# A recurrence fused with a convolutional feed-forward block on one Trainium2 core: diagonal term moved to TensorE, weight conversion in three operations, smaller loads

## The chip, the cores and the metric

The kernel runs on one core of a Trainium2 chip. The metric is the device time of one execution in microseconds. A core has five engines that run side by side and wait for each other through semaphores: TensorE (PE in the profile, its weight loads PEld), VectorE (DVE), ScalarE (ACT), GpSimd (POOL) and SyncE (SP), which issues all DMAs of this kernel in one queue.

## The reference

```
for t in range(S):                                   # B, H, S, D = 4, 8, 768, 48
    cur     = einsum('bhd,bhe->bhde', u * k[t], v[t])
    y[:,:,t]= einsum('bhd,bhde->bhe', r[t], state + cur)
    state   = w * state + einsum('bhd,bhe->bhde', k[t], v[t])
x   = y as (B, S, 384)
h   = maximum(x @ w_in, 0)                            # 384 -> 1024
c   = sum over k of conv_w[k] * h shifted by k - 1    # 3 taps along the tokens
out = (h * sigmoid(c)) @ w_out                        # 1024 -> 384
```

The weights w_in, conv_w and w_out come as float64 and are converted on the chip; r, k, v, w, u are float32.

## The kernel before, in words

**Recurrence.** Tokens go in chunks of 64; two chunks are a group of 128 tokens, a batch has 6 groups, all four batches 24. Heads go in four pairs: head A on partitions 64 to 111, head B on 0 to 47. For each group `load(g)` issues DMAs for `KR` (k and r with the head dimension on the partitions), `KRT` (k and r with the tokens on the partitions) and `WW` (the values v in blocks, with rows of zeros, beside the place of the state). `prep(g)` multiplies `KR` by powers of the decay (tables `TK`, `TR`), moves r into `RA` and `RB`, and forms the diagonal term: r times u, times k (two products over `KRT`), then a VectorE sum over the head dimension into `QQ`. GpSimd's affine select puts `QQ` on the diagonal of `RA`/`RB`. `scores(g)` ("sc" below) is 16 products into PSUM `psC`; VectorE's predicated copy puts the part below the diagonal into `RA`/`RB`. `step(g, c)` of each chunk has the state product "S" (8 products into `psS`, copied by ScalarE into the next chunk's `WW`) and the output product "av" (8 products into `psY`). `yout(g)` copies y, moves parts of it between partitions by small DMAs, and splits it into a high and a low part in `XT`.

**Feed-forward.** A batch is two units of about 384 tokens, eight units in all. Each unit has 8 steps. `first(i)`, "f1" below: nine products of 128 output features (`HP`, two PSUM buffers), then on ScalarE relu and the middle tap, on VectorE the two outer taps (`CV`), a sigmoid, the gate product (`SG`), and the split into `GH` and `GL`. `second(i)`, "f2": nine products into three output banks `PO`. So there are 64 f1 and 64 f2.

**Weights.** `convert` takes the words of a float64 as pairs of 32-bit integers. ScalarE scales the upper word read as a float (`CC`); VectorE puts the word together in `TT` with three operations: one takes the sign bit, one shifts the scaled part in, one ORs in bits of the lower word. A rounded high part and the remainder go to `wi`/`wo`. There are 17 pieces: 8 of w_in, 8 of w_out and a small one.

**Order.** `Plan` lists all operations with estimated durations and the data they read and write. A list schedule written in Python orders them before the build; it also chooses between VectorE and GpSimd for the operations marked "any". Every engine then issues its instructions in that fixed order. Where the plan has TensorE resting before the first f2, it puts in "fill" products of zeros (`wz`, 128x256, line 653; the writes go to a bank that is overwritten later). In the profile, nearly all VectorE and GpSimd products bear the line of the helper `tt`, L288.

Of the kernel before, what the change touches and what calls it, by code (L numbers as in the profile page):

```python
# [5 lines left out]
F32 = mybir.dt.float32  # L6
# [7 lines left out]
# choices of the schedule  # L14
DR = 2
# [12 lines left out]
OFF = {  # microseconds by which classes of operations come earlier  # L28
# [15 lines left out]
NBUF = 3  # L44
# [10 lines left out]
U = 386                 # most tokens of a unit of the FFN  # L55
PAT = {"2": [(0, 382), (382, 386)], "s": [(0, 384), (384, 384)]}  # units of a batch: first token, tokens
UNITS = [(b,) + x for b in range(B) for x in PAT[UP[b]]]
NU = len(UNITS)
WS = 256.0              # the weights on chip are scaled by this


class Plan:
    """Operations in a valid order, with the resources they take and the data they read and write. They are
    issued in the order of a list schedule: each engine takes, of what can start, what the tensor engine's
    sequence needs first."""
# [3 lines left out]
    def __init__(self):  # L69
        self.ops = []  # L70
        self.last_w, self.last_r = {}, {}

    def op(self, eng, dur, rd, wr, fn, cls="", x=0.0):
        """x: of a transfer, its time on the DMA engines; of matrix products, the columns they count for the clock."""
# [18 lines left out]
        self.ops.append((dur, x, sorted(pred), fn, cls))  # L93
        return n
# [18 lines left out]
    def order(self):  # L113
# [22 lines left out]
        while todo:  # L136
# [30 lines left out]
            if e == "pe":  # L167
                # zero products where the engine would rest and its clock with it
# [19 lines left out]
                if att and cls not in ATT:  # L188
                    free[e] += 0.065
# [8 lines left out]
                # the part of the block before the end of the tick  # L198
# [13 lines left out]
            elif e == "sp":  # L212
                free[e] = s + d + 0.04
                dq = max(dq, s + d + 0.65) + x
# [3 lines left out]
            else:  # L218
                free[e] = s + d
# [17 lines left out]
LAT, LPE = 0.15, 0.21  # L237
ATT = ("th", "sc", "S", "av")


def rwkv_ffn_kernel(tc, krd, krt, vt, wd, ut, w_in, conv_w, w_out, out):
# [4 lines left out]
    with ExitStack() as ctx:  # L246
# [14 lines left out]
        KRT = sb([128, 2, NP, 2, D], F32, "KRT", NBUF)  # L261
# [22 lines left out]
        def tt(eng, n, rd, wr, cls="", **kw):  # L284
            d = {"dve": dve(n), "pool": pool(n)}
            if eng != "any":
                d = {eng: d[eng]}
            op(eng, d, rd, wr, lambda e: e.tensor_tensor(**kw), cls)  # L288
# [5 lines left out]
        wz = sb([128, 512], BF16, "wz")  # L294
        wc = sb([112, NP], F32, "wc")
        uu = sb([128, NP, D], F32, "uu")
# [10 lines left out]
        dma([], ["wc"], wc, wd)  # L307

# [7 lines left out]
        def load(g):  # L316
            i = g % NBUF
            dma([], [("KR", i)], KR[i], krd[g], 0.45, 1.27, "ldK")
# [4 lines left out]
        dma([], ["uu"], uu, ut)  # L323
# [20 lines left out]
        # powers of the decay: PW[j] = w^j, TK = w^(31-j), TR = w^(j-32), DN = w^(95-j)  # L344
# [19 lines left out]
        op("dve", 0.53, ["PW"], ["PW2"], powers2)  # L364
        op("act", 0.32, ["PW", "PW2"], ["DN"], lambda e: A.copy(DN, PW[:, :, 95:31:-1]))
# [22 lines left out]
        ncv = [0]  # L388

        def convert(src, n, dst, view, keys):  # L390
# [5 lines left out]
            op("act", act(n), [("ST", i)], [("CC", i)],  # L396
               lambda e: A.activation(cc, s2[:, :, 1].bitcast(F32), AF.Copy, scale=2.0 ** -111))
# [319 lines left out]
```

## Time and profile before

| | us |
|---|---|
| median of three runs (344.40 to 347.00) | 344.52 |
| span of the profiled execution | 343.2 |
| first f1 starts in the profiled execution | 50.57 |
| TensorE's last product ends | 339.86 |
| busy: PE, DVE, ACT, POOL | 311.8, 270.4, 206.5, 193.7 |

The profile has no separate time of its execution beside the span; the median of the runs lies 1.3 us above the span, and this distance is taken for what lies around it. The page's busy times overlap: a matmul counts as busy while it goes through the array, though the next has started. The rows of one engine in order of time show how far apart starts are. Each TensorE product of float32 operands appears there as two rows.

### The profile page before, as it was taken

Reading aid. Unit: us, or ns where it says so; the run is one execution under the profiler, and the core shown is the slowest. Engines: PE = TensorE matmul, PEld = TensorE weight load, DVE = VectorE, ACT = ScalarE, POOL = GpSimd, SP = SyncE. Lnnn points to the kernel's source line nnn. Section 1 sums busy time; section 2 is a strip of 40 time slices with the busy share of each in tenths; the row PEclk is TensorE's granted clock in tenths of the full one; section 3 lists DMA queues with packets and bytes.
Section 4 is the critical chain, followed back from the end, with each engine's and each line's share of the span. In section 5 each row is a group of like instructions: output and inputs, shape, how many; then the busy total and the mean of one; then the engine's idle time right before and its main releaser. Section 6 shows DMA issues by size and latency. Waiting matters only on the chain.

```text
span 343.2 us, 8886 instructions
## 1 busy us (share of the span) xinstructions
PE 311.8 (91%) x3487; PEld 285.1 (83%) x3487; DVE 270.4 (79%) x409; ACT 206.5 (60%) x468; POOL 193.7 (56%) x200
## 2 busy tenths in 40 slices
PE   8698694997779988999998999899999999999996
PEld 4486474896668988899997999898999999999995
DVE  6899989989999999978778786786775756565550
ACT  4343446584765765567575663685566755876752
POOL 5998998697899988727455463333231212243230
PEclk9768969698998999999999999999999999999999
DMA  7996975977864297365566571544530200200101
GB/s 192 328 261 166 289 216 173 304 181 218 262 196 124 55 313 214 97 201 165 149 181 174 147 217 50 145 141 135 157 96 13 72 1 2 77 5 1 71 0 70
DMA packets 23882, 50.25 MB, mean 146 GB/s; under 512 B 4448, under 2 KB 10848, under 8 KB 23840
## 3 DMA queue, kind: packets, MB, share of 16 engines
q1 hardware_dynamic: 23840, 49.69, 50.0%
q8 instruction: 27, 0.44, 0.6%
q14 instruction: 15, 0.12, 0.1%
HBM read 36.30 MB, written 4.72 MB: 120 GB/s over the span
## 4 chain that ended last, share of the span: by engine, by line
PE 53%; DVE 17%; POOL 8%; issue 7%; DMA 7%; ACT 6%; SPq 1%; DVEq 0%; POOLq 0%; ACTq 0%
PE HP L569 20%; PE PO L598 19%; DMA KR<-in_krd_dram 4%; PE psC L477 4%; PE psY L507 3%; DVE CV L577 3%; PE psS L493 3%; POOL KRT L288 2%; DVE KR L288 2%; ACT SG L580 2%; DVE RB L481 2%; POOL RA L462 1%; DVE KRT L288 1%; DVE RA L481 1%; PE PO L653 1%
## 5 line engine op out<-in xcount | busy, mean ns | idle before, releaser
L569 PE MATMUL HP<-XT,wi 128*128 128x386 f32 (+2 forms) x576 | 116.1, 347 | 5.0 <-DVE SG L581 5.0
L598 PE MATMUL PO<-GH,wo 128*128 128x384 f32 (+2 forms) x384 | 111.6, 345 | 4.1 <-POOL wo L288 3.3
L569 PEld LDWEIGHTS HP<-XT,wi 128*128 128x128 f32 x576 | 103.4, 192 | 8.5 <-DVE SG L581 4.9
L288 POOL TENSOR_TENSOR GL<-SG,GH 128x384 fp32r<-128x384 f32 (+2 forms) x50 | 53.5, 1070 | 97.5 <-ACT GH L583 87.1
L577 DVE SCALAR_TENSOR_TENSOR CV<-HP,cw,CV 128x384 f32<-128x384 f32 (+2 forms) x128 | 78.2, 614 | 25.4 <-ACT CV L574 23.5
L598 PEld LDWEIGHTS PO<-GH,wo 128*128 128x128 f32 x384 | 71.0, 189 | 6.5 <-POOL wo L288 3.9
L598 PE MATMUL PO<-GL,wo 128*128 128x384 f32 (+2 forms) x192 | 65.3, 340 | 0.0
L580 ACT ACTIVATE SG<-CV 128x384 f32<-128x384 f32 (+2 forms) x64 | 33.5, 524 | 45.8 <-DVE CV L577 45.4
L581 DVE TENSOR_TENSOR SG<-HP,SG 128x384 f32<-128x384 f32 (+2 forms) x64 | 35.5, 555 | 21.1 <-ACT SG L580 20.4
L573 ACT ACTIVATE HP<-HP 128x386 f32<-128x386 f32 (+2 forms) x64 | 30.5, 477 | 23.2 <-PE HP L569 22.5
L583 ACT CAST GH<-SG 128x384 fp32r<-128x384 f32 (+2 forms) x64 | 32.8, 512 | 13.7 <-DVE SG L581 13.7
L500 ACT COPY WW<-psS 48x192 f32<-48x192 f32 x88 | 27.3, 311 | 20.3 <-PE psS L494 15.6
L288 DVE TENSOR_TENSOR KR<-KR,TKR 112x1024 f32<-112x1024 f32 (+1 forms) x24 | 36.2, 1509 | 3.9 <-DMA KR<-in_krd_dram 3.9
L574 ACT ACTIVATE CV<-HP,cw 128x384 f32<-128x384 f32 (+2 forms) x64 | 37.1, 579 | 1.3
L493 PEld LDWEIGHTS psS<-WW,KTA 112*48 112x48 f32 x352 | 21.6, 136 | 18.5 <-ACT WW L500 9.4
L493 PE MATMUL psS<-WW,KTA 112*48 112x48 f32 x352 | 27.2, 224 | 10.3 <-ACT WW L500 7.3
L598 PEld LDWEIGHTS PO<-GL,wo 128*128 128x128 f32 x192 | 36.5, 190 | 0.0
L507 PE MATMUL psY<-RA,WW 112*48 112x64 f32 x384 | 32.9, 233 | 0.9 <-ACT WW L500 0.9
L508 PE MATMUL psY<-RB,WW 128*48 128x64 f32 x384 | 32.4, 233 | 0.3 <-DVE RB L481 0.3
L477 PE MATMUL psC<-KR 48*64 48x64 f32 x352 | 26.2, 227 | 5.0 <-DVE RB L481 3.8
L507 PEld LDWEIGHTS psY<-RA,WW 112*48 112x48 f32 x384 | 26.5, 133 | 4.0 <-issue 2.2
L477 PEld LDWEIGHTS psC<-KR 48*64 48x64 f32 x352 | 23.1, 140 | 7.2 <-DVE RB L481 4.0
(80 smaller groups left out, 505.4 us busy)
## 6 DMA issues: line engine op xcount, KB each, us to landing
KR<-in_krd_dram SPq DMA_DIRECT2D x24, 448.0 KB, 4.6
KRT<-in_krt_dram SPq DMA_DIRECT2D x24, 384.0 KB, 5.5
WW<-in_vt_dram SPq DMA_DIRECT2D x24, 384.0 KB, 5.0
out_dram<-OS SPq DMA_DIRECT2D x18, 192.0 KB, 2.0
ST<-in_w_in_dram SPq DMA_DIRECT2D x8, 384.0 KB, 5.8
ST<-in_w_out_dram SPq DMA_DIRECT2D x8, 384.0 KB, 4.5
RA<-KR SPq DMA_DIRECT2D x22, 96.0 KB, 4.5
RB<-KR SPq DMA_DIRECT2D x22, 96.0 KB, 4.1
```

Of the source, the lines that this page charges most:

```text
L288: op(eng, d, rd, wr, lambda e: e.tensor_tensor(**kw), cls)
L477: PE.matmul(psC[0:64, n:n + C], KK[i][64:112, p, t], ra[64:112, p, t], start=True, stop=True)
L493: PE.matmul(psS[64:112, n:n + D], KTA[i][:, p, c, :], WA[i][:, p, c, :], start=True, stop=True)
L507: PE.matmul(psY[64:112, n:n + C], WA[i][:, p, c, :], RA[i][0:112, p, t], start=True, stop=True)
L508: PE.matmul(psY[0:48, n:n + C], WB[i][:, p, c, :], RB[i][:, p, t], start=True, stop=True)
L569: PE.matmul(hp, wi[a][:, j, fs], X[:, x, j, t], start=(j == 0 and k == 0), stop=(j == 2 and k == 2))
L574: op("act", act(n) + 0.05, [H_, "cw"], [("T", ti)], lambda e: A.activation(t1, hp[:, 1:n + 1], AF.Copy, scale=cw[:, 3 * f + 1:3 * f + 2]), ...
L577: op("dve", dve(n + 60), [H_, "cw"], [("T", ti)], lambda e, k=k: V.scalar_tensor_tensor(out=t1, in0=hp[:, k:n + k], scalar=cw[:, 3 * f + k ...
L580: op("act", act(n), [("T", ti)], [("SG", ti)], lambda e: A.activation(sg, t1, AF.Sigmoid))
L581: op("dve", dve(n), [H_], [("SG", ti)], lambda e: V.tensor_tensor(out=sg, in0=hp[:, 1:n + 1], in1=sg, op=ALU.mult), "GG")
L583: op("act", act(n), [("SG", ti)], [("GH", gi)], lambda e: A.copy(gh, sg))
L598: PE.matmul(PO[m][:, :n], wo[a][:, f, ms], g2[x], start=(f == 0 and k == 0), stop=(f == NF - 1 and k == 2))
```

## The change

- **Weights.** ScalarE's operation on the upper word becomes a Prelu with a slope of 2^32 for negative inputs instead of a Copy. VectorE's three operations become two: a shift of the lower word by 29, and one that shifts the scaled part by 3 and ORs it in.
- **Diagonal term.** The two products over `KRT` and the VectorE sum are gone. Instead `KP` = decayed k times decayed r (one product of 112x512 per group, "any" engine), then 16 TensorE products with one moving column, the vector `uw` = u w ("q" below), into eight free columns of `psS`, then a ScalarE copy into `QQ`.
- **Loads.** Of `krt` only the k half is loaded (`KT`, 128x384 instead of 128x768); v is loaded in two blocks of 64x384 instead of one of 128x768. Zeros that came with v are now written by GpSimd: 32 rows of each `WW` buffer once, and the state of each batch's first chunk.
- **Groups 0 and 1.** Decayed k and decayed r are two products of 112x512; ScalarE copies r into `RA` and `RB`, where VectorE had multiplied straight into them.
- **The plan.** Some of its constants and estimated durations change, and "q" joins the classes that the plan keeps together. The order on all engines, and the choice between VectorE and GpSimd, are therefore new.

```diff
@@ class Plan: order
                 if att and cls not in ATT:
-                    free[e] += 0.065
+                    free[e] += SWITCH
...
+                if e == "dve" and self.port[i]:
+                    d += SLOWER * max(0.0, min(d, free["pool"] - s))
+                if e == "pool" and free["dve"] > s:
+                    d *= SHARED
...
-LAT, LPE = 0.15, 0.21
-ATT = ("th", "sc", "S", "av")
+LAT, LPE = 0.18, 0.21
+SLOWER, SHARED, SWITCH, XFER = 0.8, 1.25, 0.19, 1.45
+ATT = ("th", "sc", "S", "av", "q")
@@ load(g)
-            dma([], [("KRT", i)], KRT[i], krt[g], 0.45, 1.1, "ldT")
-            dma([], [("Wv", i), ("WS", i, 0), ("WS", i, 1)], WW[i], vt[g], 0.45, 1.1, "ldV")
+            dma([], [("KT", i)], KT[i], krt[g, :, 0], 0.45, 0.55, "ldT")
+            dma([], [("Wv", i, "a")], WA[i][0:64], vt[g, 0:64, 0], 0.45, 0.27, "ldV")
+            dma([], [("Wv", i, "b")], WB[i][64:128], vt[g, 64:128, 1], 0.45, 0.27, "ldV")
@@ convert
-            op("act", act(n), [("ST", i)], [("CC", i)],
-               lambda e: A.activation(cc, s2[:, :, 1].bitcast(F32), AF.Copy, scale=2.0 ** -111))
-            op("dve", dve(n, 1.6), [("ST", i)], [("TT", i)], lambda e: V.tensor_scalar(
-                out=t, in0=s2[:, :, 1], scalar1=-2 ** 31, scalar2=None, op0=ALU.bitwise_and))
+            op("act", act(n), [("ST", i)], [("CC", i)], lambda e: A.activation(
+                cc, s2[:, :, 1].bitcast(F32), AF.Prelu, scale=2.0 ** -111, alpha=2.0 ** 32))
+            op("dve", dve(n, 2), [("ST", i)], [("TT", i)], lambda e: V.tensor_scalar(
+                out=t, in0=s2[:, :, 0], scalar1=29, scalar2=None, op0=ALU.logical_shift_right), port=True)
             op("dve", dve(n), [("CC", i)], [("TT", i)], lambda e: V.scalar_tensor_tensor(
                 out=t, in0=cc.bitcast(I32), scalar=3, in1=t, op0=ALU.logical_shift_left, op1=ALU.bitwise_or))
-            op("dve", dve(n), [("ST", i)], [("TT", i)], lambda e: V.scalar_tensor_tensor(
-                out=t, in0=s2[:, :, 0], scalar=29, in1=t, op0=ALU.logical_shift_right, op1=ALU.bitwise_or))
@@ prep(g)
-            tt("any", 384, ["uu"], [("KRT", i)], out=r_t, in0=r_t, in1=uu..., op=ALU.mult)
...
-            tt("any", 384, [], [("KRT", i)], cls="p", out=r_t, in0=r_t, in1=k_t, op=ALU.mult)
-            op("dve", dve(384), [("KRT", i)], [("QQ", i)], lambda e: V.tensor_reduce(
-                out=QQ[i], in_=r_t.rearrange("q p c d -> q (p c) d"), op=ALU.add, axis=AX.X))
+            tt("any", 512, [("KK", i), ("RR", i)], [("KP", g % 2)], out=kp, in0=KK[i], in1=RR[i], op=ALU.mult)
+
+            def qmm(e):
+                for p in range(NP):
+                    for c in range(2):
+                        n, t = NP * D + 2 * p + c, slice(c * C, (c + 1) * C)
+                        PE.matmul(psS[0:64, n:n + 1], kp[64:112, p, t], uw[64:112, p:p + 1], start=True, stop=True)
+                        PE.matmul(psS[64:128, n:n + 1], kp[0:48, p, t], uw[0:48, p:p + 1], start=True, stop=True)
+            op("pe", 0.4, [("KP", g % 2), ("uw", 0), ("uw", 64)], ["psAu", "psBu"], qmm, "q", 16)
+            op("act", 0.2, ["psAu", "psBu"], [("QQ", i)], lambda e: A.copy(QQ[i], psS[:, NP * D:NP * D + 2 * NP]))
@@ estimated TensorE durations
-            op("pe", 1.263, ...  "sc", 768)        -  "S": 0.495   -  "av": 0.6   -  f1: 9 * (n + 8) / 2400.0
+            op("pe", 0.5, ...  "sc", 768)          +  "S": 0.2     +  "av": 0.25  +  f1: 9 * (n + 36) / 2400.0
```

The order of instructions moves in three places that matter below. On VectorE, a piece of weights (tiles `ST`, `CC`, `TT`; the numbers are buffers) and a group's diagonal term stand as follows between the second and fourth groups, before:

```order
L450 TENSOR_REDUCE QQ_84<-KRT_81 128x8
L398 TENSOR_SCALAR TT_115<-ST_109 128x384
L398 TENSOR_SCALAR TT_116<-ST_110 128x384
L400 SCALAR_TENSOR_TENSOR TT_115<-CC_112,TT_115 128x384
L288 TENSOR_TENSOR KR_67<-KR_67,TKR 112x1024
L481 COPY_PREDICATED RA_63<-mask,psC 64x512
L481 COPY_PREDICATED RB_66<-mask,psC 64x512
L402 SCALAR_TENSOR_TENSOR TT_115<-ST_109,TT_115 128x384
L288 TENSOR_TENSOR KRT_80<-KRT_80,uu 128x384
```

and with the change:

```order
L297 TENSOR_TENSOR KR_67<-KR_67,TKR 112x1024
L505 COPY_PREDICATED RA_62<-mask,psC 64x512
L297 TENSOR_TENSOR KP_83<-KR_67 112x512
L505 COPY_PREDICATED RB_65<-mask,psC 64x512
L415 TENSOR_SCALAR TT_117<-ST_111 128x384
L297 TENSOR_TENSOR KTA_70<-KT_79,TH 64x384
L297 TENSOR_TENSOR KTB_73<-KT_79,TH 64x384
L505 COPY_PREDICATED RA_63<-mask,psC 64x512
L505 COPY_PREDICATED RB_66<-mask,psC 64x512
L417 SCALAR_TENSOR_TENSOR TT_117<-CC_114,TT_117 128x384
```

The sum of L450 and the product with `uu` are gone from VectorE, the product `KP` has come, and a piece of weights has two VectorE rows instead of three.

On TensorE, behind the twelfth f1 (f1 rows write `HP`, f2 rows `PO`, S and q rows `psS`, sc rows `psC`, av rows `psY`; of a block of like products the first two rows are shown), before:

```order
L598 MATMUL PO_124<-GH_98,wo_137 128x386
L493 MATMUL psS<-WW_77,KTA_71 48x48
L494 MATMUL psS<-WW_77,KTB_74 48x48
...
L507 MATMUL psY<-RA_62,WW_77 48x64
L508 MATMUL psY<-RB_65,WW_77 48x64
...
L477 MATMUL psC<-KR_69 64x64
L478 MATMUL psC<-KR_69 64x64
```

and with the change:

```order
L622 MATMUL PO_126<-GL_104,wo_139 128x382
L622 MATMUL PO_126<-GH_99,wo_140 128x382
L469 MATMUL psS<-uw,KP_82 64x1
L470 MATMUL psS<-uw,KP_82 64x1
...
L531 MATMUL psY<-RA_62,WW_77 48x64
L532 MATMUL psY<-RB_65,WW_77 48x64
...
L622 MATMUL PO_124<-GH_100,wo_139 128x386
```

The q products stand with an av between two parts of one f2. Counted over the whole order of TensorE, from the first f1 on: 64 f1, 64 f2 and 17 sc in both kernels; S 33 before and 36 now; av 40 and 39; q none and 17; places where TensorE leaves f1 or f2 for the recurrence 24 and 48. Ahead of the first f1: fill products 66 and 147, sc 7 and 7, S 11 and 8, av 8 and 9, q none and 7.

On SyncE, the first loads stand in this order, before:

```order
L291 DMA KR_67<-in_krd_dram 112x1024
L291 DMA uu<-in_ut_dram 128x192
L291 DMA KRT_79<-in_krt_dram 128x768
L291 DMA KR_68<-in_krd_dram 112x1024
L291 DMA KRT_80<-in_krt_dram 128x768
```

and with the change:

```order
L300 DMA KR_67<-in_krd_dram 112x1024
L300 DMA KR_68<-in_krd_dram 112x1024
L300 DMA KR_69<-in_krd_dram 112x1024
L300 DMA uc<-in_ut_dram 48x4x1 x2
L300 DMA KT_79<-in_krt_dram 128x384
L300 DMA WW_76<-in_vt_dram 64x384 x2
```

The second group's `KR` is issued right behind the first one's, and the third's ahead of the first `KT`.

More of the change, by code (lines that the diff above doesn't have):

```diff
@@ L71, in __init__, with op @@
         self.last_w, self.last_r = {}, {}
-    def op(self, eng, dur, rd, wr, fn, cls="", x=0.0):
+        self.port = []
+    def op(self, eng, dur, rd, wr, fn, cls="", x=0.0, port=False):
         n = len(self.ops)
@@ L260, in rwkv_ffn_kernel @@
         WA, WB = [x[0:112, 0] for x in WW], [x[:, 1] for x in WW]
-        KRT = sb([128, 2, NP, 2, D], F32, "KRT", NBUF)
+        KT = sb([128, NP, 2, D], F32, "KT", NBUF)
+        KP = sb([112, NP, GT], F32, "KP", 2)
         QQ = sb([128, NP * 2], F32, "QQ", NBUF)
@@ L307, in rwkv_ffn_kernel @@
         dma([], ["wc"], wc, wd)
+        for o, q in ((0, 64), (64, 0)):
+            dma([], [("uc", o)], uc[o:o + 48], ut[q].rearrange("p d -> d p"))
         def warm(e):
@@ L364, in rwkv_ffn_kernel @@
         op("dve", 0.53, ["PW"], ["PW2"], powers2)
+        for o in (0, 64):
+            op("dve", 0.1, ["wc", ("uc", o)], [("uw", o)], lambda e, o=o: V.tensor_tensor(
+                out=uw[o:o + 48], in0=uc[o:o + 48], in1=wc[o:o + 48], op=ALU.mult))
         op("act", 0.32, ["PW", "PW2"], ["DN"], lambda e: A.copy(DN, PW[:, :, 95:31:-1]))
@@ L424, in prep @@
             i = g % NBUF
-            k_t, r_t = KRT[i][:, 0], KRT[i][:, 1]
+            k_t = KT[i]
             def c2(ap, n):
@@ L449, in prep @@
-            tt("any", 384, [], [("KRT", i)], cls="p", out=r_t, in0=r_t, in1=k_t, op=ALU.mult)
-            op("dve", dve(384), [("KRT", i)], [("QQ", i)], lambda e: V.tensor_reduce(
-                out=QQ[i], in_=r_t.rearrange("q p c d -> q (p c) d"), op=ALU.add, axis=AX.X))
+                tt("dve", 1024, ["TK1", "TK2", "TR1", "TR2"], [("KK", i), ("RR", i)], "KR", out=kr, in0=kr, in1=TKR.rearrange(
+                    "q a p t -> q (a p) t").unsqueeze(2).broadcast_to([112, 2 * NP, 2, C]), op=ALU.mult)
+            else:
+                for T, W, ks, key in ((KK, TK, ["TK1", "TK2"], "KK"), (RR, TR, ["TR1", "TR2"], "RR")):
+                    tt("dve", 512, ks, [(key, i)], "KR", out=v2(T[i], 0, 112), in0=v2(T[i], 0, 112), in1=c2(W, 112), op=ALU.mult)
@@ new lines, in prep @@
+            for o, T, nm in ((64, RA, "a"), (0, RB, "b")):
+                wr = [("Rr", i, nm)] + ([("Rz", i)] if o == 0 else [])
+                if g < DR:
+                    op("act", act(512), [("RR", i)], wr, lambda e, o=o, T=T: A.copy(T[i][o:o + 48], RR[i][o:o + 48]), "Rr")
+                else:
+                    dma([("RR", i)], wr, T[i][o:o + 48], RR[i][o:o + 48], 0.625, 0.27, "rmv")
+            kp = KP[g % 2]
+            tt("any", 512, [("KK", i), ("RR", i)], [("KP", g % 2)], out=kp, in0=KK[i], in1=RR[i], op=ALU.mult)
@@ L461, in prep @@
+            if g % GPB == 0:
+                for o, T in ((64, WA), (0, WB)):
+                    op("pool", 0.35, [("Wz", i)], [("WS", i, 0)], lambda e, o=o, T=T: G.memset(T[i][o:o + 48, :, 0, :], 0.0), "WS0")
             for o, T, nm in ((0, RA, "a"), (64, RB, "b")):
```

50 lines of the change are left out of this document (19 added, 31 removed).

## Prediction

> **What bounds the kernel now.** First the table of stretches, cut where the first f1 starts (50.57 us), where the twelfth f1 ends (117.66) and where the last product ends; columns after each engine are its busy us, then the granted TensorE clock and the DMA share.
>
> ```profile
> core 0: us, PE busy (x) PEld busy (x) DVE busy (x) ACT busy (x) POOL busy (x), PEclk, DMA share, GB/s
> 0.00:50.57 50.57, 40.37 (x623) 29.74 (x623) 45.34 (x67) 21.13 (x57) 43.15 (x55) 0.80 0.85 239
> 50.57:117.66 67.09, 55.35 (x628) 48.83 (x628) 64.88 (x94) 43.17 (x96) 58.41 (x51) 0.90 0.67 196
> 117.66:339.86 222.20, 216.09 (x2239) 206.57 (x2238) 160.22 (x250) 141.70 (x315) 92.15 (x96) 1.00 0.38 110
> ```
>
> VectorE sets the pace of the first two stretches (45.3 of 50.6, 64.9 of 67.1 us busy) with GpSimd close behind; in the third it is TensorE. The ends of these stretches come from the chain that ended last and from the count of relus:
>
> ```profile
> 50.57 1.88 PE HP L569 x9
> 115.83 1.83 PE HP L569 x9
> 314.57 1.57 PE PO L598 x9
> 316.14 1.60 PE HP L569 x9
> 317.74 0.34 PE PO L598 x2
> ```
>
> ```profile
> L573 ACT ACTIVATE HP<-HP 128x384 f32<-128x384 f32 (+1 forms) x12 | 5.7, 475 | 5.0 <-PE HP L569 5.0
> ```
>
> Late in the kernel an f2 and an f1 take 317.74 - 314.57 = 3.17 us, with nothing between; that is TensorE's own pace. Next the waits of TensorE in stretch two (the longest three) and three (all):
>
> ```profile
> PE psS L493 <- ACT WW L500: 4.6, 1, 4.6
> PE PO L598 <- POOL wo L288: 3.3, 2, 2.2
> PE HP L569 <- DVE SG L581: 2.7, 2, 2.5
> ...
> PE psS L493 <- ACT WW L500: 2.7, 3, 1.3
> PE HP L569 <- DVE SG L581: 2.2, 5, 0.7
> PE psY L507 <- ACT WW L500: 0.9, 1, 0.9
> ```
>
> Stretch two has over 10.6 us of waits, mostly for weights and for gates held up on VectorE, and a clock of 0.90, a further 6.7 us. Stretch three has 5.8.
>
> **What TensorE has to do.** One group's turn, from TensorE's rows in order of time:
>
> ```profile
> 163.17 1.75 PE L569 MATMUL HP<-XT,wi 128*128 128x386 f32 x9
> 164.85 0.24 PE L493 MATMUL psS<-WW,KTA 112*48 112x48 f32 x1
> ...
> 165.02 0.21 PE L493 MATMUL psS<-WW,KTA 112*48 112x48 f32 x1
> ...
> 165.06 0.21 PE L493 MATMUL psS<-WW,KTA 112*48 112x48 f32 x1
> ...
> 165.24 0.22 PE L507 MATMUL psY<-RA,WW 112*48 112x64 f32 x1
> ...
> 165.79 0.27 PE L477 MATMUL psC<-KR 48*64 48x64 f32 x1
> ...
> 166.87 0.24 PE L493 MATMUL psS<-WW,KTA 112*48 112x48 f32 x1
> ...
> 167.81 0.44 PE L598 MATMUL PO<-GH,wo 128*128 128x384 f32 x1
> ...
> 169.48 0.34 PE L569 MATMUL HP<-XT,wi 128*128 128x386 f32 x1
> ```
>
> From start to start S takes 0.39 us, av 0.55, sc 1.08. The f1 ahead (1.68) and the f2 behind (1.67) are each about 0.1 longer than 1.60 and 1.57, so each time TensorE leaves the feed-forward costs 0.2. With the counts of the order from the first f1 on, before: 64 x 3.17 + 33 x 0.39 + 40 x 0.55 + 17 x 1.08 + 24 x 0.2 = 261 us. From 50.57 to 339.86 are 289.3 us, so **28 us are lost**, 20 of them in stretch two (its share of the work is 12 f1, 7.7 f2, 8 S, 12 av, 4 sc and 9 departures, 47 us of 67) and 8 in stretch three.
>
> **The q products.** No row shows a product with one moving column. The table products at the start have 64 weight columns and 48 moving ones:
>
> ```profile
> 6.33 0.22 PE L369 MATMUL psY<-ident,DN 48*64 48x48 f32 x1
> ...
> 6.39 0.22 PE L369 MATMUL psY<-ident,DN 48*64 48x48 f32 x1
> ```
>
> They start 0.06 us apart; S, with 48 moving columns too but 48 weight columns, 0.04 (165.02 to 165.06). Sc, 64 and 64, comes to 0.06 as well. So the 64 weight columns seem to set the pace, and q, with 64, would cost as much as sc: 1.08 us a group. Bounds: it could follow its moving column instead; then the block is near nothing but the change of kind (0.15, what sc's 1.08 has over 16 x 0.058), so 0.2; above, sc's 1.08 with the 0.2 of a departure, 1.28. I take 1.08, from the row with 64 weight columns. The Trainium skill ("TensorEngine Tiling (Array Packing)", Instruction Overhead) says that a product with one moving column takes as long as one with 60; that speaks against this change, and the 0.06 us of the table rows agree. Its "TensorE: Matmul & The Clock Gate" (Wait — 56ns, not 53.3ns?) puts the least distance of starts at about 25 ns; by that q would be an estimated 0.55 and the sum 9 us lower.
>
> The order with the change therefore asks for 64 x 3.17 + 36 x 0.39 + 39 x 0.55 + 17 x 1.08 + 17 x 1.08 (q) + 48 x 0.2 = 285, with seven fills 286 us: **25 more**, 18 for q and 5 for departures. Those 25 stand against the 28 lost.
>
> **What VectorE gets back.** Means over the first 120 us:
>
> ```profile
> L288 DVE TENSOR_TENSOR KR<-KR,TKR 112x1024 f32<-112x1024 f32 x11 | 17.9, 1628 | 0.0
> L402 DVE SCALAR_TENSOR_TENSOR TT<-ST,TT 128x384 int32<-128x384 int32 x16 | 12.5, 782 | 0.1
> L450 DVE TENSOR_REDUCE QQ<-KRT 128x8 f32<-128x384 f32 x12 | 6.5, 543 | 1.0 <-POOL KRT L288 0.9
> L288 DVE TENSOR_TENSOR KR<-KR,TKR 112x512 f32<-112x512 f32 x2 | 2.2, 1101 | 1.7 <-DMA KR<-in_krd_dram 1.7
> ...
> L288 POOL TENSOR_TENSOR KRT<-KRT 128x384 f32<-128x384 f32 x11 | 15.5, 1410 | 0.5
> ```
>
> and three single rows, the first tap of the first f1, the second tap of the twelfth, and ScalarE's smallest piece of weights:
>
> ```profile
> 57.01 0.62 DVE L577 SCALAR_TENSOR_TENSOR CV<-HP,cw,CV 128x382 f32<-128x382 f32 x1
> ...
> 122.64 0.60 DVE L577 SCALAR_TENSOR_TENSOR CV<-HP,cw,CV 128x386 f32<-128x386 f32 x1
> ...
> 35.64 0.22 ACT L406 ACTIVATE cw<-TT 128x24 f32<-128x24 f32 x1 [0.39 <-DVE TT L402]
> ```
>
> Up to the twelfth f1's second tap the list loses 17 third operations (13 us), 13 sums (7), four 384-wide KRT products (3, at some 0.7 as between the sum's row and half of the 1024-wide one) and four 48-row products into RA and RB (4, at the 512-wide row): 27. It gains five KP, which no row shows: half of the 1024-wide row is 0.81, the 512-wide row 1.10 (ends for the range: the 0.54 of the sum, 1.41 of GpSimd's row); at 0.9, 4.5 us. Four GL splits that GpSimd had are 2.4 at the tap's 0.6, two more KR products 2, the rest of the regrouping 2. Net **16 us less**. GpSimd loses most of two products a group, the one shown at 1.41, and gets at most one KP (1.4 by its row, 1.9 scaled to 512 columns) and small memsets. ScalarE gets 24 copies of 128x8; nothing of that shape is shown, the 24-column piece of weights took 0.22, and ScalarE is 43 of 67 us busy, so they hide, as does Prelu if it takes what the Copy took; both kernels' orders have two table loads. The loads that become smaller:
>
> ```profile
> KRT<-in_krt_dram SPq DMA_DIRECT2D x24, 384.0 KB, 5.5
> WW<-in_vt_dram SPq DMA_DIRECT2D x24, 384.0 KB, 5.0
> ```
>
> Half of each goes, from queues that the first stretch shows 0.85 busy; beside that stand some 25 more issues on SyncE. I cost them at zero: VectorE, not a load, fills that stretch; the one wait for a load in the rows above, 1.7 us for KR, is the most to be had, and is kept in the lower end of the first f1.
>
> **First f1.** Summed with these means, VectorE's list up to the first f1's taps is 54 us before (57 in the trace) and 53 after, because seven full weight pieces instead of five or so stand ahead of it. TensorE's list ahead of the first f1 is another matter. Twelve fills on the chain took
>
> ```profile
> 45.25 2.67 PE PO L653 x12
> 21.85 0.94 PE PO L653 x5
> ```
>
> 0.22 us each at a low clock; 256 columns at full clock are half, 0.11. Warm-up 4.8, table 0.3, 7 sc, 8 S, 9 av, 7 q and 147 fills are 45 us at full clock, where before was 29; at the granted 0.80 the new list would be 55. More fills keep the clock up, so I take 51 for the first f1, with 45 and 57 as ends.
>
> **Sum.** The twelfth f1: 53 us of work to it (12 f1, 7.3 f2, 10 S, 10 av, 4 sc, 5 q, 13 departures, fills), so 104; VectorE's second tap there stood near 122.6 and is due at 106, some 3 behind its f1, so TensorE is last. One us of waits: 105. Behind it 286 - 53 = 232.5, and 5.5 lost instead of 8.3 (VectorE has more slack, the 2.5 that the waits don't name stay): 343. Then 3.3 to the end of the span: 346.2, and 1.3 around it: **347.5 us**, 3 us or 0.9% over the median of 344.52. The front gains 12.7 us, the rest pays 16.
>
> **Rivals.**
> - *Faster*: q follows its single moving column. Then 17 x 0.88 = 15 us less behind the first f1, of which five q stand where VectorE would then be last (106 - 3 against 100): 11 to 12 come through, 336; with half of it, 341. The same sign with the first f1 at 45 instead of 51: 341.5, as VectorE holds the twelfth f1 at 103. For it: the plan's shorter TensorE times may pack the front better. Against: the 0.06 us rows.
> - *Clearly slower*: the fills become the wait. They are in fixed order; where TensorE is behind the plan when it reaches 20 or 31 of them, each delays sc and q, whose results VectorE's copies need. The plan counts sc as 0.5 and S as 0.2, the trace shows 1.08 and 0.39, so TensorE will run late. From the point where its 45 us of list plus waits pass 51, each us goes to the end: 57 for the first f1 and a clock still at 0.9 behind it give 353.5.
> - *Nothing*: VectorE's relief and TensorE's load cancel, all losses of stretch three but 2.5 vanish and the front is as reckoned: 344.
>
> **Chances.** The forecast 0.40 (own range 344 to 351), faster 0.25, clearly slower 0.20, nothing 0.15. The range takes the bounds of q (0.2 to 1.28: -12, +3) and of the first f1 (-6, +6) as far as 8 in 10 need: 338 to 355. One per cent, 3.4 us, is about what a measurement of this kernel can tell from no change. Faster by more than that: 0.25; within: 0.35 (the third rival and half of the forecast); slower: 0.40.
>
> **What would show it.** Right: rows of q start 0.06 us apart; the twelfth f1 ends near 105; TensorE's waits behind it are under 5 us; the clock is 1.00 from the first f1 on; f1 and f2 late are still 3.17 a pair. Wrong: q rows 0.01 to 0.04 apart (faster rival); the first f1 at 55 or later with fills on the chain just ahead (slower rival); a VectorE still busy over 95% to 120 us, which would mean that KP or the two remaining conversions cost more than their neighbours' rows.

## The result, and the profile after

| | before | after |
|---|---|---|
| median of the runs, us | 344.97 (4 runs, 344.4 to 347.0) | 357.27 (4 runs, 352.8 to 358.3) |
| ratio to before, 95% interval | | 1.0315 (1.0239 to 1.0391) |
| span of the profiled execution, us | 343.2 | 355.4 |
| first f1 starts | 50.57 | 61.13 |
| from there to the end of the last product | 289.29 | 290.68 |

The change makes the kernel 3.1% slower, 10 us above the forecast of 347.5 and 2 us above its range. Some executions run at a lower granted clock and take longer; the times of the experiments below leave these out (the changed kernel then has 357.07), except that all four of a_conv3 are counted. The profile places the miss. The table of stretches of the changed kernel, cut as in the prediction (first f1, end of the twelfth f1, end of the last product; busy us of each engine, then the granted TensorE clock and the DMA share):

```profile
core 0: us, PE busy (x) PEld busy (x) DVE busy (x) ACT busy (x) POOL busy (x), PEclk, DMA share, GB/s
0.00:61.13 61.13, 55.17 (x896) 42.77 (x897) 46.57 (x68) 25.47 (x68) 40.63 (x58) 0.86 0.66 183
61.13:118.93 57.80, 55.33 (x792) 49.75 (x792) 47.51 (x70) 40.38 (x96) 40.64 (x39) 0.97 0.59 175
118.93:351.81 232.88, 232.87 (x2658) 220.25 (x2658) 150.05 (x235) 142.71 (x331) 84.28 (x88) 1.00 0.28 81
```

TensorE is now busy for all but 0.01 us of the third stretch and all but 2.5 us of the second. VectorE, which set the pace of the second (64.9 of 67.1 us before), is 47.5 of 57.8 busy. The page's chain of work that ended last says the same, before and after:

```profile
PE 53%; DVE 17%; POOL 8%; issue 7%; DMA 7%; ACT 6%; SPq 1%; DVEq 0%; POOLq 0%; ACTq 0%
```

```profile
PE 89%; DVE 5%; ACT 3%; issue 1%; POOL 1%; DMA 0%; ACTq 0%; DVEq 0%
```

The account of TensorE's time, an estimate in us (idle is a stretch minus PE busy, the clock's loss is PE busy times one minus the granted clock, both from the rows above and those of before):

| | front: before, after | from the first f1 on: before, after |
|---|---|---|
| idle | 10.2, 6.0 | 17.9, 2.5 |
| clock | 8.1, 7.7 | 5.5, 1.7 |
| busy, at full clock | 32.3, 47.4 | 265.9, 286.5 |

Behind the first f1 the change gets 19 us of waits and clock back and pays 21 us of work. In the front it gets 4.6 back and pays 15: 7 blocks of q, and zero products. Their groups in the trace of before and of the changed kernel (recorded rows, busy us, mean ns):

```profile
L653 PE MATMUL PO<-wz 128*128 128x256 bf16 x67 | 12.9, 342 | 0.0
```

```profile
L677 PE MATMUL PO<-wz 128*128 128x256 bf16 x154 | 24.1, 310 | 0.0
```

TensorE hardly waits any more. These are all of its waits behind the first f1:

```profile
PE psS L469 <- ACT WW L524: 1.5, 1, 1.5
PE psS L517 <- ACT WW L524: 0.7, 1, 0.7
PE psC L501 <- DVE RB L505: 0.2, 1, 0.2
```

Next TensorE's rows of one q block, between an f2 and an av:

```profile
166.16 0.34 PE L622 MATMUL PO<-GH,wo 128*128 128x384 f32 x1
166.43 0.21 PE L469 MATMUL psS<-uw,KP 48*64 48x1 f32 x1
...
166.51 0.19 PE L469 MATMUL psS<-uw,KP 48*64 48x1 f32 x1
166.52 0.19 PE L470 MATMUL psS<-uw,KP 48*64 48x1 f32 x1
166.57 0.19 PE L469 MATMUL psS<-uw,KP 48*64 48x1 f32 x1
...
167.46 0.26 PE L531 MATMUL psY<-RA,WW 112*48 112x64 f32 x1
```

The rows of one tile position (L469) stand 0.06 us apart, those of L470 run beside them, and the block takes 1.03 us, though each product has one moving column. The new and changed operations elsewhere cost little (groups of the page: busy, mean ns):

```profile
L297 DVE TENSOR_TENSOR KP<-KR 112x512 f32<-112x512 f32 x10 | 8.4, 838 | 0.1
L297 POOL TENSOR_TENSOR KP<-KR 112x512 f32<-112x512 f32 x14 | 19.0, 1360 | 18.3 <-DVE KR L297 12.2 <-PE psY L532 5.6
L413 ACT ACTIVATE CC<-ST 128x384 f32<-128x384 f32 x16 | 8.9, 556 | 0.0
L472 ACT COPY QQ<-psS 128x8 f32<-128x8 f32 x24 | 4.0, 165 | 21.2 <-PE psS L470 21.2
```

### The profile page after: what moved, and what is told of

It is laid out like the page before. It is cut to its first block, busy times and chain, and to the rows that moved or that the text cites. A ratio compares the mean times of both kernels' runs of the same rounds, so it can differ in the third digit from the quotient of the medians.

```text
span 355.4 us, 10623 instructions
## 1 busy us (share of the span) xinstructions
PE 343.4 (97%) x4342; PEld 312.8 (88%) x4342; DVE 244.1 (69%) x372; ACT 209.0 (59%) x496; POOL 165.6 (47%) x183
## 4 chain that ended last, share of the span: by engine, by line
PE 89%; DVE 5%; ACT 3%; issue 1%; POOL 1%; DMA 0%; ACTq 0%; DVEq 0%
PE PO L622 30%; PE HP L593 30%; PE psC L501 6%; PE psS L469 6%; PE psY L531 6%; PE psS L517 5%; PE PO L677 3%; DVE KR L297 1%; PE psS L470 1%; DVE TT L415 1%; DVE TT L417 1%; ACT WW L524 1%; PE psY L532 1%; PE psC L502 1%; PE psS L518 1%
## 5 line engine op out<-in xcount | busy, mean ns | idle before, releaser
L622 PE MATMUL PO<-GH,wo 128*128 128x384 f32 (+2 forms) x384 | 115.1, 348 | 0.0
L593 PE MATMUL HP<-XT,wi 128*128 128x386 f32 (+2 forms) x576 | 114.3, 344 | 0.0
L297 POOL TENSOR_TENSOR GL<-SG,GH 128x384 fp32r<-128x384 f32 (+2 forms) x40 | 42.2, 1056 | 82.8 <-ACT GH L607 62.3
L604 ACT ACTIVATE SG<-CV 128x384 f32<-128x384 f32 (+2 forms) x64 | 33.6, 525 | 32.7 <-DVE CV L601 32.3
L505 DVE COPY_PREDICATED RA<-mask,psC 64x512 f32<-64x512 int32 x24 | 17.5, 730 | 28.0 <-PE psC L502 27.1
L297 DVE TENSOR_TENSOR KR<-KR,TKR 112x1024 f32<-112x1024 f32 (+1 forms) x26 | 33.6, 1299 | 3.0 <-DMA KR<-in_krd_dram 2.2
L486 POOL TENSOR_SCALAR_AFFINE_SELECT RA<-QQ 64x512 f32<-64x512 f32 x24 | 18.1, 754 | 36.1 <-ACT QQ L472 35.4
L501 PE MATMUL psC<-KR 48*64 48x64 f32 x384 | 28.8, 228 | 3.6 <-DVE KR L297 3.4
L469 PEld LDWEIGHTS psS<-uw,KP 48*64 48x64 f32 x384 | 25.0, 138 | 7.3 <-issue 1.8
L531 PE MATMUL psY<-RA,WW 112*48 112x64 f32 x384 | 31.1, 224 | 0.1
L501 PEld LDWEIGHTS psC<-KR 48*64 48x64 f32 x384 | 25.5, 141 | 6.0 <-DVE KR L297 4.1
```

The costliest lines, as they stand in the source:

```text
L297: op(eng, d, rd, wr, lambda e: e.tensor_tensor(**kw), cls, port=True)
L469: PE.matmul(psS[0:64, n:n + 1], kp[64:112, p, t], uw[64:112, p:p + 1], start=True, stop=True)
L501: PE.matmul(psC[0:64, n:n + C], kk[64:112, p, t], rr[64:112, p, t], start=True, stop=True)
L531: PE.matmul(psY[64:112, n:n + C], WA[i][:, p, c, :], RA[i][0:112, p, t], start=True, stop=True)
L593: PE.matmul(hp, wi[a][:, j, fs], X[:, x, j, t], start=(j == 0 and k == 0), stop=(j == 2 and k == 2))
L604: op("act", act(n), [("T", ti)], [("SG", ti)], lambda e: A.activation(sg, t1, AF.Sigmoid))
```

## Experiments

Each kernel was timed against the kernel before on the same chip; a ratio is to that. The kernels a_noq, a_noqf and a_noqb leave a part of the diagonal out and only serve to price it.

| | kernel | us | ratio, 95% interval |
|---|---|---|---|
| a_noq | changed, no q products | 334.94 | 0.971 (0.966 to 0.975) |
| a_noqf | changed, no q ahead of the first f1 | 350.65 | 1.019 (1.013 to 1.025) |
| a_noqb | changed, no q behind it | 339.86 | 0.987 (0.983 to 0.991) |
| a_q4 | changed, 4 larger q products a group | 350.68 | 1.018 (1.012 to 1.024) |
| a_conv3 | changed, old conversion | 358.67 | 1.043 (1.038 to 1.049) |
| a_nofill | changed, no zero products | 361.09 | 1.047 (1.044 to 1.050) |
| a_petimes | changed, old planned TensorE times | 392.00 | 1.139 (1.132 to 1.147) |
| a_oldplan | changed, all plan constants old | 400.38 | 1.161 (1.156 to 1.165) |
| a_true | changed, attention planned as traced | 349.25 | 1.013 (1.006 to 1.020) |
| b_newplan | before, new plan | 345.42 | 1.001 (0.997 to 1.006) |
| b_weights | before, new conversion | 349.68 | 1.015 (1.011 to 1.019) |
| b_v | before, v in blocks | 348.35 | 1.011 (1.007 to 1.014) |
| b_weights_v | before, both, old plan | 351.36 | 1.019 (1.016 to 1.022) |
| b_wnew | before, new conversion, new plan | 341.44 | 0.991 (0.987 to 0.994) |
| a_sum | changed, diagonal back on VectorE | 335.99 | 0.977 (0.970 to 0.985) |
| a_sum_true | the same, attention planned as traced | 338.67 | 0.982 (0.977 to 0.986) |

**What q costs: a_noq.** The loop of q products goes.

```diff
-                for p in range(NP):
-                    for c in range(2):
-                        ... two products
+                pass
```

> The changed kernel in its own order, with the 24 x 16 small q products left out and their eight columns of psS set to zero once (the diagonal term of the attention is missing). KP, the copy to QQ and all else stay. Theory W (TensorE's added work is the cause, wherever it stands): 24 blocks of 1.08 us are 26 us; the zero products and waits take some of that back, and the time falls by 18 to 26 us, to 331 to 339. Theory F (the front, to the first f1, is set by the other engines, and only what stands behind it counts): the first f1 stays at 58 to 61, and of the 17 blocks behind it 18 us come through: 338 to 341. Theory O (the order or the conversions are the cause and the q's fill time that TensorE would have lost anyway): the time falls by less than 10 us, to 347 or more.

334.94: 22.1 us under the changed kernel (22.3 between the medians of all executions), as theory W had it. The windows up to the first f1 and from there on:

```profile
0.00:53.13 53.13, 42.63 (x672) 32.31 (x673) 47.54 (x69) 25.04 (x68) 41.11 (x59) 0.95 0.73 204
53.13:329.50 276.37, 271.57 (x2903) 252.28 (x2902) 201.71 (x305) 182.85 (x427) 126.23 (x125) 1.00 0.37 106
```

The first f1 comes 8.0 us earlier, which theory F had not expected, and 14.3 us are gained behind it. Of 24 blocks of 1.03 us, 24.7, the kernel pays 22.1.

**Front and back apart: a_noqf, a_noqb.** The same loop is kept for some groups.

```diff
-                for p in range(NP):
+                for p in range(NP if g >= 7 else 0):     # a_noqf
+                for p in range(NP if g < 7 else 0):      # a_noqb
```

> The changed kernel in its own order, with the q products of the first seven groups alone left out, those that stand ahead of the first f1 (their part of the diagonal term is missing). Theory F (TensorE's list ahead of the first f1, the q blocks in it, sets the first f1): the first f1 starts at 52 to 55 instead of 61, and the time falls by 6 to 9 us, to 348 to 351. Theory G (those blocks stand where TensorE would wait for VectorE and the copies anyway): the first f1 stays at 58 to 61 and the time at 354 to 358.

> The changed kernel in its own order, with the q products of the other 17 groups left out, those behind the first f1 (their part of the diagonal term is missing). Theory W: 17 blocks of 1.08 us are 18.4; the first f1 stays at 60 to 62 and the time falls by 13 to 18 us, to 339 to 344, with losses of 0 to 5 us coming back as VectorE gets later against TensorE. Theory G: nearly all of the 22.3 us that leaving out all q blocks gave comes from here, 335 to 338.

350.65 and 339.86: 6.4 and 17.2 us under the changed kernel, 23.6 together where leaving out all gave 22.1. Windows of a_noqf, then of a_noqb:

```profile
0.00:53.84 53.84, 42.15 (x672) 31.89 (x673) 46.62 (x68) 25.00 (x68) 40.07 (x58) 0.97 0.73 198
53.84:347.80 293.96, 291.37 (x3448) 272.75 (x3446) 197.95 (x306) 182.97 (x428) 126.09 (x126) 0.98 0.35 101
```

```profile
0.00:60.31 60.31, 52.07 (x896) 41.03 (x897) 45.69 (x69) 25.70 (x68) 41.23 (x58) 0.91 0.67 186
60.31:337.80 277.49, 272.13 (x2903) 252.55 (x2902) 200.25 (x304) 182.59 (x427) 126.46 (x126) 1.00 0.36 104
```

Seven blocks in the front hold the first f1 up by 7.3 us, their own length (7 x 1.03 = 7.2). They did not stand in waits: theory F. The other 17 cost 17.2 of their 17.5 us: theory W.

**What sets q's price: a_q4.** The weights become 128 columns wide, the products a quarter as many.

```diff
-    PE.matmul(psS[0:64, n:n + 1], kp[64:112, p, t], uw[64:112, p:p + 1], ...)   # 16 a group
-    PE.matmul(psS[64:128, n:n + 1], kp[0:48, p, t], uw[0:48, p:p + 1], ...)
+    PE.matmul(psS[:, n:n + 2], kp[:, p, :], uw2[:, p, :], ...)                  # 4 a group
```

> The changed kernel with its q block written as 4 products instead of 16: for each head pair all 112 rows and 128 tokens of KP are the weights, and the moving operand has two columns (the weights u of one head each, zero in the other's rows). Result as before; the copy to QQ becomes four copies of 64 x 4, since the second chunk lands on the other half of the rows. Theory W, with the pace set by the weight columns (0.06 us for a pair of 64): 4 products at 0.06 to 0.12 us and 0.15 for the change of kind are 0.4 to 0.65 a block instead of 1.08, 24 blocks give 10 to 16 us back, 7 to 12 of them behind the first f1: 343 to 349. If a product costs by its moving columns alone, the 16 would not have cost 1.08, so the block of 4 near 0.2 would only say that the count of products sets the price: 338 to 341. Theory O: 354 to 359, as the changed kernel. The three more copies on ScalarE (0.17 us each) are hidden unless the affine selects of GpSimd wait for them.

350.68: no theory's number. The shape of a block tells why the gain of theory W did not come (the profiled execution took 359.95 us, so only a block is read from it; the granted clock is 1.00 from 155 to 158 us). The end of av, the block's eight rows, two a product:

```profile
155.84 0.22 PE L536 MATMUL psY<-RA,WW 112*48 112x64 f32 x1
155.85 0.22 PE L537 MATMUL psY<-RB,WW 128*48 128x64 f32 x1
156.00 1.05 PE L475 MATMUL psS<-uw,KP 112*128 112x2 f32 x8
```

The next sc starts at 156.98, so eight rows take 0.98 us, 0.12 each, twice the 0.06 of a pair with 64 weight columns. The count of products does not set the price. Nor do the moving columns, though they went from one to two: the rows of sc in the kernel before, with 64 weight and 64 moving columns, stand 0.06 us apart like q's. What fits all three is the weight columns that pass, and they are as many as before. My sum had taken 4 rows of 0.06 to 0.12 us; there are eight, two a product, at 0.12. Blocks shorter by 0.05 us give back 1.2 us; the interval (1.012 to 1.024) just touches that of the changed kernel (1.024 to 1.039), and whether some 5 us more were gained elsewhere isn't known.

**The zero products: a_nofill.**

```diff
                 if i < 0:
-                    PE.matmul(PO[2][:, :FN], wz[:, :128], wz[:, :FN], start=True, stop=True)
+                    pass
```

> The changed kernel with all 147 zero products that its plan puts between the early blocks left out of what is issued; every other instruction keeps its place (zero products feed no output). Theory P (the plan's zero products stand in TensorE's fixed order and push the first f1 back): 10.6 us of them lie on the chain before the first f1 at 61.1, so the first f1 starts at 51 to 55 and the time falls to 347 to 352. Theory V (what the first f1 needs is late on VectorE, ScalarE and the copies; the zero products only stand where TensorE would wait): the first f1 stays at 60 to 62, or comes 1 to 3 us later because the clock falls, and the time is 356 to 361. The work behind the first f1 is the same under both, some 290 us with its losses.

361.09, slower by 4 us: theory V, just past its upper end. The front without them:

```profile
0.00:62.23 62.23, 43.71 (x749) 37.73 (x749) 44.14 (x68) 25.14 (x67) 37.05 (x57) 0.60 0.65 181
```

The granted clock falls from 0.86 to 0.60, a loss of 17.5 us instead of 7.7, and idle time goes from 6.0 to 18.5. So the zero products as a whole are not what holds the front up: their time comes back as clock.

**The plan: a_oldplan, a_petimes, a_true.** All operations are those of the changed kernel; only numbers that set the order differ.

```diff
 # a_oldplan, both groups; a_petimes, the second alone (new -> old)
-LAT, LPE = 0.18, 0.21; SLOWER, SHARED, SWITCH, XFER = 0.8, 1.25, 0.19, 1.45
+LAT, LPE = 0.15, 0.21; SLOWER, SHARED, SWITCH, XFER = 0.0, 1.0, 0.065, 1.0
-sc 0.5, S 0.2, av 0.25, q 0.4; f1 and f2: n + 36 columns
+sc 1.263, S 0.495, av 0.6, q 1.263; f1 and f2: n + 8 columns
 # a_true
+sc 0.95, S 0.37, av 0.48, q 0.95; f1 and f2: n + 36 columns
```

> The changed kernel with the constants of the plan of before: latencies, no surcharge for the shared port, switch 0.065, and the planned TensorE times 1.263 (sc), 0.495 (S), 0.6 (av), and 1.263 for q instead of 0.4. Operations are all those of the changed kernel. Theory P (the new constants order the front badly): the first f1 returns to 50 to 54, and with 286 us of TensorE work and 4 to 6 us of losses behind it the time is 345 to 349. Theory W (TensorE's 286 us of work are the cause, and the order ahead of the first f1 hardly depends on the constants): the first f1 stays at 58 to 62 and the time at 354 to 359.

> The changed kernel with one group of plan constants set back: the planned TensorE times (1.263 for sc and q, 0.495 for S, 0.6 for av, the old ones for f1 and f2), which are near what the trace shows; latencies, port surcharge, switch and transfer factor stay new. It lies between the changed kernel (357) and that with all old constants (400). Theory T (the short planned times are what packs the front with zero products and keeps the clock up): 380 to 400, with fewer than 60 zero products and a mean clock under 0.92. Theory U (latency and port constants do it): 352 to 362, since TensorE's order follows its dependences and true times cost nothing.

> The changed kernel with its planned TensorE times for the attention set to what the trace shows (sc and q 0.95 beside the switch of 0.19, S 0.37, av 0.48); those of f1 and f2 and all other constants stay new. Theory T (the plan needs short times: with true ones it sees TensorE busy, puts in few zero products and the clock falls): under 60 zero products ahead of the first f1, a mean clock under 0.93, 375 to 395. Theory S (the losses of the kernel with the old TensorE times, 394, came from the old times of f1 and f2, short by 0.1 us each against the attention's): 350 to 362.

400.38: both expectations missed. 392.00: as theory T said. 349.25: theory S, a little better. The zero products' group of a_petimes and its windows, cut near its first f1:

```profile
L677 PE MATMUL PO<-wz 128*128 128x256 bf16 x8 | 1.9, 360 | 0.0
```

```profile
0.00:64.00 64.00, 48.60 (x789) 40.59 (x789) 58.48 (x86) 33.38 (x84) 44.45 (x62) 0.60 0.82 225
64.00:390.90 326.90, 305.33 (x3410) 289.66 (x3408) 197.75 (x302) 178.62 (x412) 100.66 (x107) 0.92 0.28 79
```

The same of a_true:

```profile
L677 PE MATMUL PO<-wz 128*128 128x256 bf16 x99 | 13.6, 277 | 0.0
```

```profile
0.00:52.66 52.66, 45.57 (x907) 35.89 (x907) 49.55 (x69) 27.56 (x73) 38.71 (x58) 0.96 0.69 197
52.66:343.90 291.24, 286.13 (x3382) 269.60 (x3381) 201.83 (x305) 183.99 (x423) 121.08 (x124) 0.99 0.36 102
```

With the old times the plan puts in almost no zero products: the front runs at a clock of 0.60, and the order behind it loses 21.6 us idle and 24 to the clock. With the attention's times of the trace the first f1 starts at 52.66, 8.5 us earlier than in the changed kernel, with 907 recorded TensorE products ahead of it instead of 896, and the rest takes 0.6 us longer (291.24 against 290.68): 8 us of the 12 are a matter of the plan's numbers. At full clock TensorE's work in the front is 43.7 us instead of 47.4, and idle time and clock take 8.9 instead of 13.7. Whether 55 zero products fewer do it, or the other order that came with them, isn't separated; nor is it known which of the numbers that a_petimes has beside a_true's does the harm.

**The other parts, alone and together: b_newplan, b_weights, b_v, b_weights_v, b_wnew.** Each is the kernel before with the parts that its row in the table names. The lines of each part:

```diff
 # new conversion
-   A.activation(cc, ..., AF.Copy, scale=2.0 ** -111)
+   A.activation(cc, ..., AF.Prelu, scale=2.0 ** -111, alpha=2.0 ** 32)
-   three VectorE operations: sign, scaled part, lower word
+   two: lower word shifted by 29; scaled part shifted by 3 and ORed in
 # v in blocks
-   dma([], [("Wv", i), ...], WW[i], vt[g], ...)
+   dma([], [("Wv", i, "a")], WA[i][0:64], vt[g, 0:64, 0], ...)
+   dma([], [("Wv", i, "b")], WB[i][64:128], vt[g, 64:128, 1], ...)
+   memsets on GpSimd for the zeros that came with v
 # new plan: constants and planned TensorE times of the changed kernel
```

> The kernel before with the plan constants of the changed one (latencies, the surcharge for the port, switch 0.19, transfers times 1.45, and the planned TensorE times 0.5, 0.2 and 0.25), and none of its new operations. Theory P: the same constants that made the changed kernel's front late do it here, the first f1 goes from 50.6 to 55 to 61 and the time to 348 to 355. Theory W: the order of the front is set by VectorE's work, the first f1 stays within 2 us of 50.6, and the time is 342 to 347.

> The kernel before with one part of the change alone: weight words converted by one Prelu and two VectorE operations instead of a Copy and three. Seventeen third operations of 0.78 us go, 13 us of VectorE's list up to the twelfth f1. Theory C (VectorE's list sets the first two stretches of before, so its relief comes through where TensorE had 20 us to lose): the twelfth f1 ends 6 to 12 us earlier than 117.7 and the time is 333 to 339. Theory N (the weights wait for their copies or for GpSimd, not for VectorE; or the plan moves other work into the gap): 342 to 346. A Prelu that took longer than the Copy (0.55 us) would show as ScalarE rows of over 0.6 us.

> The kernel before with one part of the change alone: v loaded as the two blocks that are used, 192 KB instead of 384 KB a group, with memsets on GpSimd for what the load brought as zeros (r stays loaded whole). Theory N (no load sets the first stretch): 343 to 346. Theory L (the queues, 0.85 busy in the first 50 us, hold the loads of KR up): the 1.7 us wait for KR goes and the time is 340 to 343; the memsets on GpSimd, some 6 us of a list 43 of 50 us busy, may cost 1 to 3 us instead.

> The kernel before with both of the change's reliefs (Prelu and two operations for the weights, v in two blocks) and the old plan; the diagonal stays on VectorE. It has the operations of the kernel that ran in 336 us, and differs from it by the plan's constants alone. Theory C (the constants make the relief usable: without them the list schedule fills VectorE's free time with what GpSimd did, and the plan puts too few zero products in): 345 to 351, as either relief alone gave with the old plan (348.6 and 349.7). Theory R (the two reliefs only work together): 334 to 340.

> The kernel before with the conversion by Prelu and two operations and the new plan's constants, v and r loaded whole. It differs from the kernel that ran in 336 us by the load of v alone. Theory C: 335 to 341, as the loads hide. Theory L (the smaller load of v carries the gain): 342 to 347, as the kernel before with the new plan alone (346.9).

b_newplan: 345.42, within theory W's range and no difference that can be told; but the first f1 goes to 72.7, even later than theory P's 55 to 61. Its windows (of an execution of 349.84 us):

```profile
0.00:72.70 72.70, 58.30 (x825) 43.05 (x826) 63.30 (x91) 26.13 (x67) 54.12 (x63) 0.88 0.71 216
72.70:344.40 271.70, 267.26 (x2811) 252.60 (x2809) 204.90 (x325) 179.35 (x400) 133.28 (x133) 0.98 0.43 125
```

VectorE has been busy for 63.3 us by then instead of 45.3, and behind it TensorE is idle for 4.4 us instead of 17.9. So a late first f1 alone need not be a loss: here the other engines got work done meanwhile for which TensorE waits later in the kernel before.

b_weights: 349.68: both theories missed, a relief of VectorE made the kernel 1.5% slower. Its page:

```profile
PE 309.5 (89%) x3511; PEld 286.7 (83%) x3511; DVE 266.3 (77%) x411; ACT 208.2 (60%) x468; POOL 172.2 (50%) x181
```

Third operations worth 13 us are gone, but VectorE's busy time falls by 4 (from 270.4) and GpSimd's by 21.5 (from 193.7): the list schedule gave VectorE products that GpSimd had (GpSimd has 181 operations instead of 200). TensorE's idle time to its last product goes from 28.1 to 33.7 us. b_v (348.35) lies above both theories' ranges; the memsets' 1 to 3 us would account for it, but that wasn't tried. Both reliefs with the old plan (351.36) are slower too, as theory C said, just past its upper end. With the new plan the same parts gain: 341.44 with the conversion (again just past theory C's upper end), 335.99 with v as well (a_sum below, which has these parts and no others).

**The diagonal undone: a_sum, and with the trace's times: a_sum_true.** The lines for the diagonal of before stand in place of q, KP and the loads of k alone, and groups 0 and 1 are treated as before too; a_sum_true has three other planned times.

```diff
-   kp = KK * RR; 16 products psS <- kp, uw; A.copy(QQ[i], psS[:, 192:200])
+   r_t = r_t * uu; r_t = r_t * k_t; V.tensor_reduce(QQ[i], r_t, add)
 # a_sum_true
-sc 0.5, S 0.2, av 0.25
+sc 0.95, S 0.37, av 0.48
```

> The changed kernel with one part undone: the diagonal term is multiplied out on VectorE or GpSimd and summed on VectorE as before (so r is loaded whole again), while the conversion by Prelu and two operations, the smaller load of v and the constants of the new plan stay. Theory W: TensorE has 288 us of work instead of 314, VectorE 24 sums of 0.54 and two products of 384 more a group; the losses go up again by some 10 us, and the time is 338 to 345. Theory O: the conversions and the order stay as they are in the changed kernel, and so does the time, 352 to 358.

> The fastest kernel so far (336 us: the changed one with the diagonal back on VectorE), planned with the attention's TensorE times of the trace as a_true was (sc 0.95, S 0.37, av 0.48). Theory T2 (true times stop zero products from being put where TensorE is in fact late, which gave the changed kernel 8 us): some 100 fewer zero products ahead of the first f1, and 328 to 334. Theory W2 (that gain came because TensorE was the bound in the changed kernel's front; here VectorE is, and zero products only fill waits): 334 to 339.

335.99, better than theory W had it; 2.3% faster than before and the fastest version that computes everything. Its windows:

```profile
0.00:61.94 61.94, 50.13 (x781) 38.37 (x781) 54.48 (x81) 25.77 (x66) 55.08 (x71) 0.97 0.79 226
61.94:330.40 268.46, 266.30 (x2837) 250.81 (x2837) 203.05 (x319) 178.73 (x401) 132.51 (x134) 0.99 0.40 115
```

Its first f1 is as late as in the changed kernel, and it still ends 21 us earlier, because 268 us follow instead of 291. The 24 sums and 48 products that went back to VectorE and GpSimd lie beside TensorE's work. a_sum_true is at 338.67, as theory W2 had it: without q the true times gain nothing that can be told.

**The conversion within the changed kernel: a_conv3.** The part "new conversion" above, undone in the changed kernel.

> The changed kernel with the conversion of the weights undone (a Copy and three VectorE operations a piece), the diagonal on TensorE, the smaller loads and the new plan kept. Theory W (TensorE is the limit, 26 us of q on it; VectorE has slack from the first f1 on): seven third operations before the first f1 are 5.5 us there and the rest hides: 357 to 364. Theory V (the conversions bound the first two stretches of the changed kernel too): all 17 of 0.78 us come through, 366 to 372.

358.67 (353.45 to 362.05): theory W's number, far under theory V's, and with overlapping intervals no difference from the changed kernel that can be told. W's path isn't shown: the profiled execution, of 353.45 us, has the first f1 at 55.1, earlier and not later, and 293.3 us behind it. A price of the third operation beside TensorE's load doesn't show here, and the new order that came with it isn't separated.

## Why the prediction was wrong

The sign of the likeliest case was right, the size was not.

- **The step that failed: the first f1 at 51 ("More fills keep the clock up, so I take 51", ends 45 and 57).** It started at 61.13, outside both ends. The list ahead of it was sized well: 45 us at full clock forecast, 47.4 came. The 6 us left for losses were the term too small, and they had no row: the front of before had lost 18.3 us (10.2 idle, 8.1 clock), the changed one lost 13.7. The clock rose only from 0.80 to 0.86, but a higher clock would not have saved the forecast: a_noqb has the same list ahead of the first f1, its clock there was 0.91, and the first f1 came at 60.31, since idle time grew from 6.0 to 8.2 us as the clock's loss fell from 7.7 to 4.7. In the order of the changed kernel, with its zero products, the two come to about 13 us together each time (13.7; a_noqb 12.9, a_noqf 13.0, a_noq 12.6, with clocks of 0.86 to 0.97), in that of a_true to 8.9. They belong to the order; what in it makes them stays open. My own figure with the old clock, 55 us, was nearer, and idle time belonged on top of it.
- **The mechanism of the "clearly slower" rival was half right.** It said that TensorE, planned at 0.5 for a block of 1.08, falls behind and then works through zero products that it doesn't need, and put the first f1 at 57 and the time at 353.5. a_true fits it: planned with the trace's times, 55 zero products fewer, the first f1 at 52.66 and 8 us less, though the zero products aren't separated there from the rest of the order. a_nofill shows that the zero products as a whole are needed; the rival's price was 4 us short.
- **From the first f1 to the last product: right.** Forecast 346.2 - 3.3 - 51 = 291.9, measured 290.7. Within it the two terms of losses were off in both directions: 4.2 us lost to the twelfth f1 instead of 1, none instead of 5.5 in stretch three. That they partly cancel is luck. The clock in stretch two was 0.97, not 1.00.
- **q at 1.08 us: right** in size and place; a_noq, a_noqf and a_noqb show that nearly every block, in front and behind, lengthens the kernel by its own length. The *faster* rival falls with it. The Trainium skill's "TensorEngine Tiling (Array Packing)", Instruction Overhead (one moving column as long as 60), spoke against a gain from the narrow operand, and the rows agree that there is none; but if the moving side set the price, a_q4's rows with two moving columns would be no longer than q's with one, and they took twice as long, 0.12 us. By the 25 ns that the Trainium skill's "TensorE: Matmul & The Clock Gate" (Wait — 56ns, not 53.3ns?) gives as the least distance of starts, q would be an estimated 0.55 us, half of the 1.03 that came.
- **VectorE's list: right.** Up to the twelfth f1 it is 46.57 + 47.51 = 94.1 us busy instead of 110.2, 16 less as forecast; KP took 0.84 on VectorE (0.9 taken) and 1.36 on GpSimd, the Prelu 556 ns, the copy to QQ 165 ns and hidden.
- **The *nothing* rival** had late losses vanish, which they did, but needed the same front.

What the change does, as the runs show it: it moves work from an engine that has slack for two thirds of the kernel to one that has none. Its conversions and smaller load of v are worth 9 us with the new plan (345.4 to 336.0), its diagonal on TensorE, with the loads and the treatment of groups 0 and 1 that go with it, costs 21 (336.0 to 357.1), of which 8 can be had back by planning with the times of the trace.

## What to carry to other kernels

Where one engine is busy for nearly all of a stretch, its added work is paid in full, by the block's whole length on that engine and not by what it computes; move work only toward the engine that idles in that stretch. Size a stretch that is still bound by several engines by the losses it has, idle and clock, and let none of them go without a row that says why. A planner's numbers are part of the kernel: the same relief lost 2% with one set of constants and gained 2% with another, so test a change together with its plan, and each part alone.

## What the runs showed of the hardware

- A product of float32 operands costs by its weight columns when the moving operand is narrow: 0.06 us a row for a pair of 64 columns with one moving column (`after`), 0.12 for 128 columns with two (a_q4). When it is not narrow, its columns count as well: with 48 weight columns the rows of S (48 moving columns) stand 0.04 us apart, those of av (64) 0.06. S is shown in the prediction; av, in the kernel before:

```profile
165.24 0.22 PE L507 MATMUL psY<-RA,WW 112*48 112x64 f32 x1
...
165.30 0.22 PE L507 MATMUL psY<-RA,WW 112*48 112x64 f32 x1
...
165.36 0.22 PE L507 MATMUL psY<-RA,WW 112*48 112x64 f32 x1
```

- Zero products moved the mean granted clock of the front from 0.60 to 0.86 in the same order, and their time came back in full: without them (a_nofill) the kernel was 4 us slower.
- A Prelu of 128x384 takes 556 ns, as the Copy in its place (552 ns in the trace of before).
